# A chunked attention with two MLP layers on one core: the V cast, its write and its gathers stand five to six plan steps further back

## Chip, cores and metric

The kernel runs on one core of a Trainium2 chip. The metric is the device time of one execution in microseconds (us); a time is the median of several runs. Engines are named as in the profile: PE is TensorE (matmuls), PEld its weight loads, DVE VectorE, ACT ScalarE, POOL GpSimd, SP SyncE, whose DMA queue issues the loads, writes and transposes.

## The reference

Three parts follow one another: chunked attention, a leaky MLP, and a sigmoid-gelu MLP. All inputs are float32.

```python
def _attn_ref(q, k, v, mem_k, mem_v):          # 4 batches, 8 heads, 768 rows, 64 wide; 8 memory rows
    ...
    for c in range(nc):                        # chunks of 32 rows
        l_start = max(0, c_start - 16)
        r_end = min(S, c_end + 8)
        k_full = np.concatenate([mem_k, k[:, :, l_start:r_end]], axis=2)
        v_full = np.concatenate([mem_v, v[:, :, l_start:r_end]], axis=2)
        scores = scale * np.matmul(q_c, k_full.transpose(0, 1, 3, 2))
        a = np.exp(scores - np.max(scores, axis=-1, keepdims=True))
        a = a / (np.sum(a, axis=-1, keepdims=True) + 1e-09)
        out[:, :, c_start:c_end] = np.matmul(a, v_full)

def _moe_ref(x, w_in, w_out, alpha):           # 3072 tokens, 512 -> 2048 -> 512
    h = x @ w_in
    return (np.maximum(h, 0.0) + alpha * np.minimum(h, 0.0)) @ w_out

def _moe2_ref(x, w_in, w_out):
    h = x @ w_in
    return (h * (1.0 / (1.0 + np.exp(-1.702 * h)))) @ w_out
```

## The kernel before

**Numbers.** A float32 operand is split into a high and a low half of float16, and a product is made of three float16 products. `cast_hi` (L126) makes the high half on ACT, `sub_lo` (L129) the low half on DVE. The scale of each operand comes from its largest magnitude: `absmax` (L123) on DVE, a pass on ACT that writes to `junk` (L325) for K and Q, and `all_max` (L118 and L119), a small product `mx` on PE and a maximum `ar` on DVE.

**Tiles.** The 3072 tokens are 12 blocks of 256. The first MLP layer runs block by block: a step has a `mlp_g1` (L569: 24 matmuls into `h`), an activation on ACT (L604: `h` to `t`), a DVE part (L607: `t` and `h` to `gf`), the split of `gf` in halves (`g`), and a `mlp_g2` (L649: 24 matmuls into `acc`) for an older `h`. When a block of the MLP is done, `acc` is copied out as `yf` (L685). The weights of both layers are decoded while this runs (`w_load`, L150 and L152; `w_dec`, L191 to L204; `w_sub`, L227; `w_op`, L237 to L239, where `wh` is cast on ACT, combined on POOL and written by SP).

**Attention between the steps.** The attention of a token block stands between the MLP steps of earlier blocks. It loads `kf`, `qf` and `vf` (`att_load`, L300 to L316), finds their maxima, casts K, Q and V, transposes K into `kt` (`att_tk`, L448) and Q (`att_tq`, L434) by DMA, swaps the halves of Q (`att_swap`, L440 and L441), writes V to DRAM as `v_dr` (`att_vw`, L454) and gathers it from there into `vbd` in the form that the product needs, two gathers a head (`att_vr`, L463 and L464). Then come the scores (`att_qk`, L472 and L473), their copy `sc` on ACT (`att_ext`, L487 and L489), the softmax, its transposition to `aT` by DMA (`att_ta`, L525), and two output products `xp` (`att_pv`, L538), whose halves `xt` are the input of the MLP. All of `kf`, `qf`, `vf` and `vbd` are single tiles, used by one block after the other, and so is `kt`. The high and low halves of K and of V are tiles with the same tag, `kv16`, of a pool with one buffer:

```python
        kt = at_p.tile([128, H, 304], F16, tag="kt", name="kt")
        for g, n in ((0, 128), (1, 128), (2, 48)):
            nc.sync.dma_start_transpose(out=kt[:, :, g * 128:g * 128 + n], in_=k16[0:n, g].rearrange("p h t d -> p (h t d)"))
```

A matmul result of `h`, `xp`, `mx` and of `acc` takes one of five PSUM banks.

**What sets the order.** Blocks 0 and 1 have their attention in float32, and that of block 2 is placed by hand (`start`). For blocks 3 to 11 the table `ATT` gives each piece a plan step, relative to the block. Three plan steps belong to one MLP step, and a block has 24. The table writes the program's order only: each engine's own order is then made from it by the scheduler of the framework, so that a piece may end up before or behind work near it. "Block 7" below is the stretch in which K, Q and V of attention block 7 are cast; the two `xp` that stand beside that V cast belong to the block before, and the scores of block 7 follow.

Of the kernel before, what the change touches and what calls it, by code (L numbers as in the profile page):

```python
# [36 lines left out]
def kernel(  # L37
# [15 lines left out]
    B, H, S, D = q.shape  # L53
# [747 lines left out]
    def run_plan(t):  # L801
# [9 lines left out]
        (-7, att_load, 1), (-6, att_load, 0), (-5, att_load, 2),  # L811
        (0, att_max, 1), (1, att_max, 0), (1, att_max, 2), (2, att_all, 0, 3), (4, att_scale, 0, 3),
        (5, att_hi, 1), (6, att_lo, 1), (6, att_hi, 0), (8, att_tk), (7, att_lo, 0), (9, att_tq),
        (9, att_hi, 2), (10, att_lo, 2), (12, att_vw), (13, att_swap),
        *[(15 + h // 2, att_vr, h) for h in range(H)],
        (18, att_qk, 0), (18, att_ext, 0), (20, att_smax, 0), (21, att_qk, 1), (21, att_ext, 1),
        (22, att_exp, 0), (23, att_smax, 1), (24, att_sum, 0), (25, att_exp, 1), (26, att_a16, 0),
        (27, att_sum, 1), (28, att_ta, 0), (29, att_a16, 1), (31, att_ta, 1),
# [222 lines left out]
```

## Time and profile before

| what | value |
| --- | --- |
| median of 3 runs | 1219.28 us (1215.82 to 1219.78) |
| the profiled execution | 1217.3 us, its span 1215.5 us |
| mean granted clock of TensorE, as a share of full speed | 0.946 |
| PE busy | 1086.0 us (89%) |
| DVE busy | 850.9 us (70%) |
| ACT busy | 632.8 us (52%) |
| POOL busy | 632.5 us (52%) |

The page and the trace come from one profiled execution. A span is the time from the first to the last instruction; the execution's own time lies a little above it. Busy shares are averages over stages with different limits, so that the waits of each stage have to be read in its own rows. The attention blocks 3 to 11 lie in the first 680 us. In a row of the timeline, the bracket at the end says how long the engine had been idle before and what it was waiting for; "SPq" is SP issuing a DMA. PEclk of a window is the share of the full clock that TensorE was granted.

### The profile page before, as it was taken

The page shows a single profiled execution, that of the slowest core. Times are in us where ns is not written, and L with a number is a line of the kernel's source. Part 1 is how long each engine was busy: PE and PEld are TensorE (multiplying, and loading weights), DVE is VectorE, ACT ScalarE, POOL GpSimd, SP SyncE. Part 2 cuts the span into 40 slices and gives each one's busy share as a digit, 9 for nine tenths or more (in the row PEclk, how much of TensorE's full clock was granted, in tenths as well). Part 3 has the DMA queues.
Part 4 walks back from the last instruction along what each step waited for, and adds up shares of the span by engine and source line. Part 5 has one row for each costly group of instructions (what it writes and reads, how often), then busy time and mean ns, then how long its engine had stood idle before and what let it go on. Part 6 is the DMA issues. An engine that isn't in the chain of part 4 may idle for free.

```text
span 1215.5 us, 25510 instructions
## 1 busy us (share of the span) xinstructions
PE 1086.0 (89%) x10294; PEld 955.8 (79%) x10294; DVE 850.9 (70%) x1509; ACT 632.8 (52%) x968; POOL 632.5 (52%) x740
## 2 busy tenths in 40 slices
PE   3677879899979898898989999989999898999998
PEld 2665768788869797787979988778788687787887
DVE  6898894687869686776957347767666665766672
ACT  4567546564747556564745344555544544444442
POOL 1244641233607153442607046696876968868763
PEclk8678889999989898998989999999999999999999
DMA  9958238597886969687764515110100100100001
GB/s 204 306 121 187 81 105 159 105 235 162 212 164 194 178 178 219 148 212 168 205 128 126 231 53 233 45 53 10 44 19 19 40 15 18 36 5 15 19 18 36
DMA packets 241318, 142.97 MB, mean 118 GB/s; under 512 B 200176, under 2 KB 220656, under 8 KB 240176
## 3 DMA queue, kind: packets, MB, share of 16 engines
q1 hardware_dynamic: 241200, 141.34, 46.3%
q8 instruction: 81, 1.33, 0.5%
q14 instruction: 37, 0.30, 0.1%
HBM read 86.19 MB, written 33.16 MB: 98 GB/s over the span
## 4 chain that ended last, share of the span: by engine, by line
PE 28%; DVE 24%; POOL 22%; ACT 9%; DMA 7%; issue 6%; SPq 3%; ACTq 0%; POOLq 0%; DVEq 0%
PE h L569 11%; POOL ga L614 10%; PE acc L649 9%; DVE g L129 6%; POOL o L777 4%; PE acc L663 3%; POOL yt L742 3%; ACT g L126 3%; DMA kt<-k 3%; PE x L580 3%; SPq L448 2%; DVE gf L607 2%; DVE wr L204 2%; ACT v L126 2%; DVE wr L198 1%
## 5 line engine op out<-in xcount | busy, mean ns | idle before, releaser
L569 PE MATMUL h<-xt,wbig 128*128 128x256 f16 x2304 | 290.7, 287 | 50.8 <-DVE gf L607 34.0
L569 PEld LDWEIGHTS <-wbig 128*128 128x128 f16 x2304 | 236.1, 103 | 89.8 <-DVE gf L607 34.7
L649 PE MATMUL acc<-g,wbig 128*128 128x256 f16 x2304 | 271.3, 275 | 3.1 <-POOL g L632 1.5
L614 POOL TENSOR_TENSOR ga<-ga 128x128 f32<-128x128 f32 x384 | 212.8, 578 | 114.6 <-DVE ga L612 109.0
L580 PE MATMUL x<-yt,w2i 128*128 128x256 f16 x2016 | 238.1, 275 | 20.2 <-POOL yt L742 12.0
L649 PEld LDWEIGHTS <-wbig 128*128 128x128 f16 x2304 | 226.1, 99 | 31.1 <-issue 3.1
L663 PE MATMUL acc<-w2o,g 128*128 128x256 f16 x2016 | 233.9, 274 | 5.7 <-DVE g L129 2.5
L580 PEld LDWEIGHTS <-w2i 128*128 128x128 f16 x2016 | 198.2, 99 | 50.8 <-issue 20.4
L663 PEld LDWEIGHTS <-g 128*128 128x128 f16 x2016 | 197.5, 98 | 31.7 <-DVE g L129 3.4
L129 DVE SCALAR_TENSOR_TENSOR g<-ga,gk,g 128x896 f16<-128x896 f32 x96 | 122.7, 1289 | 111.3 <-ACT g L126 110.8
L126 ACT ACTIVATE g<-ga,gk 128x896 f16<-128x896 f32 x96 | 98.2, 1036 | 95.1 <-POOL ga L614 95.1
L607 DVE SCALAR_TENSOR_TENSOR gf<-t,oma,h 128x256 f32<-128x256 f32 x192 | 83.1, 473 | 69.5 <-ACT t L604 69.3
L604 ACT ACTIVATE t<-h 128x512 f32<-128x512 f32 x96 | 56.6, 590 | 91.4 <-PE h L569 77.2
L129 DVE SCALAR_TENSOR_TENSOR g<-gf,gk,g 128x512 f16<-128x512 f32 x81 | 82.9, 1024 | 1.8 <-ACT g L126 1.8
L238 POOL TENSOR_TENSOR wh<-wr,wh 128x512 f16<-128x512 f32 x24 | 37.9, 1592 | 79.6 <-ACT wh L237 79.6
L777 POOL TENSOR_TENSOR o<-o 128x256 f32<-128x256 f32 x77 | 74.7, 984 | 6.5 <-ACT o L772 6.0
L227 POOL TENSOR_TENSOR wt<-wr 128x512 f32<-128x512 f32 x16 | 24.2, 1516 | 90.4 <-DVE wr L204 90.2
L611 ACT ACTIVATE ga<-ha,l2t 128x512 f32<-128x512 f32 x48 | 34.4, 717 | 62.6 <-DVE ha L592 62.6
L213 POOL TENSOR_TENSOR wbig<-wr,wbig 128x1024 f16<-128x1024 f32 x16 | 37.1, 2326 | 52.9 <-ACT wbig L208 52.9
L126 ACT ACTIVATE g<-gf,gk 128x512 f16<-128x512 f32 x81 | 57.8, 714 | 0.4 <-DVE gf L607 0.4
L489 ACT COPY sc<-sps 32x504 f32<-32x504 f32 (+2 forms) x112 | 56.2, 502 | 1.0
L612 DVE SCALAR_TENSOR_TENSOR ga<-ga,ha 128x512 f32<-128x512 f32 x48 | 40.1, 834 | 21.9 <-ACT ga L611 21.9
(184 smaller groups left out, 1476.9 us busy)
## 6 DMA issues: line engine op xcount, KB each, us to landing
w<-in_moe_w_in_dram SPq DMA_DIRECT2D x10, 1024.0 KB
w<-in_moe_w_out_dram SPq DMA_DIRECT2D x10, 1024.0 KB
vbd<-v_dr SPq DMA_DIRECT2D x80, 112.0 KB
w2i_dr<-wh SPq DMA_DIRECT2D x28, 256.0 KB
w2o_dr<-wh SPq DMA_DIRECT2D x28, 256.0 KB
w2i<-w2i_dr SPq DMA_DIRECT2D x4, 1792.0 KB
w2o<-w2o_dr SPq DMA_DIRECT2D x4, 1792.0 KB
qf<-in_q_dram SPq DMA_DIRECT2D x24, 256.0 KB
```

What stands on the lines that cost most here:

```text
L126: nc.scalar.activation(out=hi, in_=src, func=ACTF.Copy, scale=s)
L129: nc.vector.scalar_tensor_tensor(out=lo, in0=src, scalar=s, in1=hi, op0=ALU.mult, op1=ALU.subtract)
L489: nc.scalar.copy(d[32 * c:32 * c + 32, ..., 0:WIN], x[32 * c:32 * c + 32, ..., bo + CH * c:bo + CH * c + WIN])
L569: nc.tensor.matmul(out=hp[:, e], lhsT=w[:, wt, o:o + 128], rhs=x[:, xh, kk], start=(n == 0), stop=(n == 3 * KT - 1))
L580: nc.tensor.matmul(out=xs[bank][:, i], lhsT=w[:, o, wt, kk * 256 + c:kk * 256 + c + 128], rhs=yt[sb, yi][:, yh, kk], start=(n == 0), stop= ...
L604: nc.scalar.activation(out=t, in_=hp, func=ACTF.Relu, scale=-1.0)
L607: nc.vector.scalar_tensor_tensor(out=g[:, e], in0=t[:, e], scalar=oma[:, f:f + 1], in1=hp[:, e], op0=ALU.mult, op1=ALU.add)
L612: nc.vector.scalar_tensor_tensor(out=t, in0=t, scalar=1.0, in1=hp, op0=ALU.add, op1=ALU.mult)
L614: nc.gpsimd.tensor_tensor(out=g[:, out_], in0=g[:, x], in1=g[:, y], op=op)
L649: nc.tensor.matmul(out=acc[layer, b][dt // 2][:, dt % 2 * TB:(dt % 2 + 1) * TB], lhsT=w[:, wt, dt * 128:(dt + 1) * 128], rhs=g16[:, gh, e] ...
L663: nc.tensor.matmul(out=acc[layer, b][bank][:, i * 256:(i + 1) * 256], lhsT=g16[:, gh, gs], rhs=w[:, o, wt, p % 2], start=(p == 0 and n == ...
L777: e.tensor_tensor(out=ov[:, out_], in0=ov[:, x], in1=ov[:, y], op=op)
```

## The change

Four entries of the table `ATT` get other plan steps: `att_hi` and `att_lo` of V (9 and 10 become 15 and 16), `att_vw` (12 becomes 18) and the `att_vr` gathers (from 15 becomes from 20). `att_swap` stays at 13, and so now comes ahead of the write of V. Nothing is added or removed, and blocks 0 to 2 are not placed by this table.

```diff
         (5, att_hi, 1), (6, att_lo, 1), (6, att_hi, 0), (8, att_tk), (7, att_lo, 0), (9, att_tq),
-        (9, att_hi, 2), (10, att_lo, 2), (12, att_vw), (13, att_swap),
-        *[(15 + h // 2, att_vr, h) for h in range(H)],
+        (15, att_hi, 2), (16, att_lo, 2), (18, att_vw), (13, att_swap),
+        *[(20 + h // 2, att_vr, h) for h in range(H)],
         (18, att_qk, 0), (18, att_ext, 0), (20, att_smax, 0), (21, att_qk, 1), (21, att_ext, 1),
```

The order that was built from it, engine by engine, is shown at four places. The first pair is ACT in block 7, before, from the cast of Q (`q`) on; `v` is the V cast, `t` and `g` belong to the MLP, and `xt` is the input of a later MLP block.

```order
L126 ACTIVATE q_4826<-qf,blk_143 128x16x64
L604 ACTIVATE t<-h 128x512
L126 ACTIVATE g_4948<-gf,gk_149 128x512
L126 ACTIVATE v_4954<-vf,blk_143 128x1536
L604 ACTIVATE t<-h 128x512
L126 ACTIVATE xt<-xp 128x4x128
L126 ACTIVATE g_5063<-gf,gk_149 128x512
L126 ACTIVATE xt<-xp 128x4x128
L604 ACTIVATE t<-h 128x512
```

The same place of ACT in the change:

```order
L126 ACTIVATE q_4826<-qf,blk_143 128x16x64
L237 CAST wh<-wt 128x512
L604 ACTIVATE t<-h 128x512
L126 ACTIVATE g_4948<-gf,gk_149 128x512
L604 ACTIVATE t<-h 128x512
L126 ACTIVATE v_5131<-vf,blk_143 128x1536
L126 ACTIVATE g_5060<-gf,gk_149 128x512
L126 ACTIVATE xt<-xp 128x4x128 x2
L604 ACTIVATE t<-h 128x512
```

The V cast now stands behind a second `t`; in blocks 9 and 11 it does too. In blocks 4, 6, 8 and 10 it does not. This is ACT in block 8, before:

```order
L126 ACTIVATE q_5607<-qf,blk_144 128x16x64
L604 ACTIVATE t<-h 128x512
L126 ACTIVATE g_5729<-gf,gk_149 128x512
L126 ACTIVATE v_5735<-vf,blk_144 128x1536
L604 ACTIVATE t<-h 128x512
L126 ACTIVATE xt<-xp 128x4x128
```

And ACT in block 8 in the change:

```order
L126 ACTIVATE q_5607<-qf,blk_144 128x16x64
L604 ACTIVATE t<-h 128x512
L126 ACTIVATE g_5729<-gf,gk_149 128x512
L126 ACTIVATE v_5922<-vf,blk_144 128x1536
L604 ACTIVATE t<-h 128x512
L126 ACTIVATE xt<-xp 128x4x128
```

Only the buffer's number differs. The third pair is the DMA queue of SP in block 8, before, from the first swap of Q on: the write of V (`v_dr`), the second swap, the memory rows of `kf` for the next block, `qf`, and the gathers into `vbd`.

```order
L440 DMA q_5886<-q_5733 64x2048
L454 DMA v_dr_101<-v_5735 128x1024 x2
L454 DMA v_dr_101<-v_5735 32x1024
L441 DMA q_5886<-q_5733 64x2048
L313 DMA kf<-in_mem_k_dram 8x8x64
L316 DMA kf<-in_mem_k_dram 8x8x64
L300 DMA qf<-in_q_dram 128x8x64 x2
L464 DMA vbd<-v_dr_101 8x8x128
L463 DMA vbd<-v_dr_101 56x8x128 x2
```

The queue of SP in the change, from the same swap on:

```order
L440 DMA q_5880<-q_5733 64x2048
L441 DMA q_5880<-q_5733 64x2048
L313 DMA kf<-in_mem_k_dram 8x8x64
L316 DMA kf<-in_mem_k_dram 8x8x64
L454 DMA v_dr_101<-v_5922 128x1024 x2
L454 DMA v_dr_101<-v_5922 32x1024
L300 DMA qf<-in_q_dram 128x8x64 x2
L312 DMA vf<-in_v_dram 104x8x64
L312 DMA vf<-in_v_dram 128x8x64
L312 DMA vf<-in_v_dram 32x8x64
L313 DMA vf<-in_mem_v_dram 8x8x64
L463 DMA vbd<-v_dr_101 56x8x128
```

The write stands behind the memory rows of `kf`, and the four loads of `vf` stand ahead of the sixteen gathers; before, they stood behind the last of them. The fourth pair is DVE in block 8's tail, where `vf` of block 9 gets its maximum (`blk_145<-vf`) between the parts of the weight decoding (`wr`) and the MLP (`gf`, `g`). Before:

```order
L198 SCALAR_TENSOR_TENSOR wr<-w_5613,wr 128x1024
L197 TENSOR_SCALAR wr<-wr 128x1024
L607 SCALAR_TENSOR_TENSOR gf<-t,oma,h 128x256 x2
L204 SCALAR_TENSOR_TENSOR wr<-w_5613,wr 128x1024
L129 SCALAR_TENSOR_TENSOR g_6012<-gf,gk_149,g_6012 128x512
L198 SCALAR_TENSOR_TENSOR wr<-w_5642,wr 128x1024
L607 SCALAR_TENSOR_TENSOR gf<-t,oma,h 128x256 x2
L204 SCALAR_TENSOR_TENSOR wr<-w_5642,wr 128x1024
L129 SCALAR_TENSOR_TENSOR g_6107<-gf,gk_149,g_6107 128x512
L123 TENSOR_REDUCE blk_145<-vf 128x1
L499 TENSOR_REDUCE mx<-sc 128x8
```

DVE in the change, from the same first row on:

```order
L198 SCALAR_TENSOR_TENSOR wr<-w_5613,wr 128x1024
L123 TENSOR_REDUCE blk_145<-vf 128x1
L197 TENSOR_SCALAR wr<-wr 128x1024
L607 SCALAR_TENSOR_TENSOR gf<-t,oma,h 128x256 x2
L204 SCALAR_TENSOR_TENSOR wr<-w_5613,wr 128x1024
L129 SCALAR_TENSOR_TENSOR g_5997<-gf,gk_149,g_5997 128x512
```

The maximum over `vf` now comes right behind the first L198, ahead of both pairs of `gf`.

## Rows read from the trace of the kernel before

**Rows 1.** the page, busy time of an engine: us (share of the span) xinstructions

```profile
PE 1086.0 (89%) x10294; PEld 955.8 (79%) x10294; DVE 850.9 (70%) x1509; ACT 632.8 (52%) x968; POOL 632.5 (52%) x740
```

**Rows 2.** the table of waits: engine, line, releaser: us in total, times, longest

```profile
ACT v L126 <- DMA kt<-k: 50.6, 10, 6.9
...
PE h L569 <- DVE gf L607: 34.0, 7, 5.8
```

**Rows 3.** timeline of ACT, block 7: start, us, engine, line, operation, [idle before <-releaser]

```profile
401.48 2.07 ACT L126 ACTIVATE v<-vf,blk 128x1536 f16<-128x1536 f32 x1 [6.63 <-DMA kt<-k]
403.42 0.56 ACT L604 ACTIVATE t<-h 128x512 f32<-128x512 f32 x1
```

**Rows 4.** timeline of DVE, block 7

```profile
405.40 0.86 DVE L607 SCALAR_TENSOR_TENSOR gf<-t,oma,h 128x256 f32<-128x256 f32 x2
```

**Rows 5.** timeline of PE, block 7

```profile
400.61 1.35 PE L538 MATMUL xp<-aT,vbd 128*128 128x32 f16 x48
406.32 4.89 PE L569 MATMUL h<-xt,wbig 128*128 128x256 f16 x24 [4.36 <-DVE gf L607]
```

**Rows 6.** timelines of PE, blocks 9 and 11

```profile
515.21 5.06 PE L569 MATMUL h<-xt,wbig 128*128 128x256 f16 x24 [4.64 <-DVE gf L607]
...
625.16 4.70 PE L569 MATMUL h<-xt,wbig 128*128 128x256 f16 x24 [4.60 <-DVE gf L607]
```

**Rows 7.** the chain that ended last: start, us, what

```profile
468.38 2.62 PE h L569 x24
```

**Rows 8.** windows: us, busy time of each engine, PEclk is the granted clock

```profile
297.00:302.00 5.00, 3.56 (x31) 2.83 (x30) 4.96 (x12) 1.75 (x4) 0.51 (x1) 1.00 0.97 178
407.00:412.00 5.00, 5.00 (x31) 3.80 (x30) 1.20 (x3) 0.70 (x2) 0.00 (x0) 0.64 0.88 231
```

**Rows 9.** timeline of ACT, block 5

```profile
294.07 2.06 ACT L126 ACTIVATE v<-vf,blk 128x1536 f16<-128x1536 f32 x1 [3.93 <-DMA kt<-k]
```

**Rows 10.** timeline of PE, block 5

```profile
291.48 1.35 PE L538 MATMUL xp<-aT,vbd 128*128 128x32 f16 x48
...
295.30 2.78 PE L649 MATMUL acc<-g,wbig 128*128 128x256 f16 x24
...
299.41 0.49 PE L118 MATMUL mx<-eye,wa 128*128 128x128 f32 x2 [1.33 <-DVE xt L129]
...
300.01 2.78 PE L569 MATMUL h<-xt,wbig 128*128 128x256 f16 x24
```

**Rows 11.** timelines of ACT and PE, the tail of block 5

```profile
305.46 1.48 ACT L325 ACTIVATE junk<-kf 128x1536 f16<-128x1536 f32 x1 [6.71 <-DMA kf<-in_mem_k_dram]
...
316.94 0.23 PE L472 MATMUL sps<-kt,q 128*128 128x160 f16 x1 [2.57 <-ACT sc L489]
...
341.56 1.35 PE L538 MATMUL xp<-aT,vbd 128*128 128x32 f16 x48 [0.97 <-DVE ar L119]
```

**Rows 12.** timeline of SP's DMA issues, block 8, and one of block 9

```profile
460.86 2.02 SPq L454 DMA_DIRECT2D v_dr<-v  x3
...
466.34 0.78 SPq L464 DMA_DIRECT2D vbd<-v_dr  x1
...
473.80 2.64 SPq L312 DMA_DIRECT2D vf<-in_v_dram  x3
...
476.49 0.35 SPq L313 DMA_DIRECT2D vf<-in_mem_v_dram  x1
...
500.99 1.54 SPq L525 DMA_TRANSPOSE aT<-a  x1
```

**Rows 13.** timeline of PE, beside the V cast of block 6

```profile
345.37 1.35 PE L538 MATMUL xp<-aT,vbd 128*128 128x32 f16 x48
```

**Rows 14.** timeline of DVE, block 8's tail

```profile
473.00 1.23 DVE L198 SCALAR_TENSOR_TENSOR wr<-w,wr 128x1024 uint32<-128x1024 uint32 x1
```

**Rows 15.** the chain that ended last, two landings

```profile
302.63 2.65 DMA kf<-in_mem_k_dram
...
426.53 7.50 DMA w<-in_moe_w_in_dram
```

## The prediction

> **What bounds the kernel.** I read the page's busy shares first. TensorE (PE) is busy for 1086.0 us, 89% [rows 1], so the time can change only through what PE still waits for, or through the clock at which it runs. I then read the table of waits: the longest wait of PE under one name is `h` (the first product of the MLP, L569) waiting for `gf` on DVE: 34.0 us in seven waits. Its partner is ACT's V cast waiting for the transfer of `kt`, 50.6 us in ten [rows 2]. Third came the timelines, to see that the two are one thing. In block 7 ACT stands idle for 6.63 us until the K transposes have landed, casts V for 2.07 us and only then takes `t` of the next `h` [rows 3]. DVE takes the low half of V, and the `gf` that PE needs follows only at 405.40 [rows 4]. PE has the second output product `xp` of the block before from 400.61 on and starts `h` at 406.32, after 4.36 us of idleness [rows 5]. Blocks 9 and 11 show the same, with 4.64 and 4.60 us [rows 6]. Why V waits for K: both halves' tiles have the tag `kv16` in a pool with one buffer, so the cast may write only when the transposes have read K.
>
> The wait costs more than its idle time. The `h` behind it takes 4.89, 5.06 and 4.70 us for its 24 matmuls [rows 5, 6], where the chain has 2.62 us for the same 24 elsewhere [rows 7]. The granted clock right behind the stall of block 7 is 0.64, that is, TensorE spent much of the stretch at 1.2 GHz [rows 8]. One stall of the three thus costs 4.36 + 2.27, 4.64 + 2.44 and 4.60 + 2.08 us.
>
> **The change, part by part.** The four lines of the table move the V cast and its low half by six plan units, the write by six and the gathers by five. In the order that was built from it:
>
> *Blocks 7, 9 and 11, the V cast.* It now stands behind a second `t` (the first pair of listings, block 7). ACT then waits for `kt` with that `t` already done, and PE has its next `h` and `acc` to run. Removed: idleness 4.36 + 4.64 + 4.60 = 13.60 us and slow clock 2.27 + 2.44 + 2.08 = 6.79 us, together 20.39 us.
>
> *What stands there instead.* The trace has a sample: in block 5 of the kernel before, V already stands behind the second `t` and waits 3.93 us for `kt` [rows 9]. There PE goes on from `xp` to `h` and `acc`, which follow without idleness, and only then waits 1.33 us for `xt` on DVE. The `acc` of 295.30 has issued at 295.30 + 2.62 = 297.92, and the next `h` starts at 300.01 [rows 10]: 2.09 us, in which the small product `mx` also runs. The clock stays at 1.00 over this wait [rows 8]. Three times 2.09 is 6.27 us to take off the gain.
>
> *Given back later.* In block 5 the ACT work behind it is late: the maximum over `kf` waits until 305.46 for the load of the memory rows; later PE waits 2.57 us for the scores' copy on ACT and 0.97 us for a maximum on DVE before the output products [rows 11]. That is 3.54 us which a stalled block does not have. In the changed order part of it has a remedy: on the DMA queue of SP the three writes of V (2.02 us) no longer stand ahead of the memory rows of `kf` [rows 12] (third pair of listings). I take 3.54 − 2.02 = 1.5 us for each of blocks 7 and 9, 3.0 in all. Block 11 prepares no later attention block. Bounds: 0, and 3.54 × 2 = 7.1.
>
> *Block 5 itself* keeps V behind the `t` and gets the same remedy: a gain between 0 and 2.0, since the late tail may be refilled by something else; I take 1.0.
>
> *Blocks 4, 6, 8 and 10, the V cast.* It keeps its place ahead of `t` (second pair of listings), so their stalls stay: 0.
>
> *The write and the gathers.* The sixteen gathers of V into `vbd` run on SP from 466.34 to the first load of `vf` at 473.80 [rows 12]. They now come after the loads of `vf`, so the loads go 7.4 us earlier and the gathers later by the 3.0 us that the four loads issue, and by little else. The output products that read them stand shortly ahead of the `h` of 515.21 [rows 6], over 20 us later: 0. Behind the write on SP stand the loads of `qf` and `vf`. The swaps of `q` and the memory rows go ahead of it, so V's low half has that much more time to be ready, and SP need not stand still for it: 0.
>
> *Transposes.* In block 9 the second transpose of the softmax `aT` (1.54 us of issue for such a one, [rows 12]) now stands between K transposes, and in block 5 too. That delays V, which has cover, and the second output product, which has none: 0 to 1.5 us each. I take 0.5 each, 1.0 in all.
>
> Sum: −20.39 + 6.27 + 3.0 − 1.0 + 1.0 = −11.1 us. From the profiled execution of 1217.3 us (its span is 1215.5) that is 1206.2; the median of the runs, 1219.28, is 2.0 above the profiled one, so the forecast is 1208. After the attention blocks PE runs without such waits, so everything behind shifts together.
>
> With the bounds: the largest gain is −20.39 + 6.27 − 2.0 = −16.1; the smallest, with all of the tail given back and `aT` late twice, is −20.39 + 6.27 + 7.1 + 3.0 = −4.0. Hence 1203 to 1215 for this case, on the median's scale.
>
> **Rivals.**
>
> *The gain is given back (0.22).* The hard evidence against my sum is the period of block 5. From the second `xp` beside its V, at 291.48, to that beside the next block's V, at 345.37 [rows 10, 13] are 53.89 us, and from there to 400.61 [rows 5] 55.24 us with a stall. The block without the stall is only 1.35 us shorter, where a stall of 7 less 2.09 would make it 5. If blocks 7 and 9 behave so, they bring 1.35 each, and block 11, which has no such tail, 4.60 + 2.08 − 2.09 = 4.6: together −7.3, with 1.0 either way for the rest: 1211 to 1213. Against it: the first of block 5's late waits goes back to the load of the memory rows, which the change moves.
>
> *The slower clock stays (0.06).* If the 1.33 us of idleness is enough for the clock to fall each time, 6.8 us of the gain stay away: 1215. Block 5 speaks against it, at 1.00 in the stretch of the wait [rows 8]. The Trainium skill (page "TensorE: Matmul & The Clock Gate", section "A second HAM failure mode: psum-queue depth-cycling") says that short idles between groups of matmuls, as PSUM banks are cycled, can be enough to make the clock go back and forth. Block 5's row does not bear it out here: its short idle left the clock up.
>
> *Slower (0.12): DVE is held by the loads of V.* The maximum over `vf` now stands directly behind the first L198 of the weight decoding and ahead of `gf` (fourth pair of listings); before, it stood behind two pairs of `gf`. By block 8's rows DVE comes to it at 473.00 + 1.23 = 474.2 [rows 14]. The loads of `vf` now start at 466.34 and their four issues take 3.0 us [rows 12], to 469.3. With a landing like the 2.65 us of the memory rows of `kf` they are there at 472.0 and nothing waits; with one like the 7.50 us of a weight load they come at 476.8 [rows 15], and DVE, with `gf` behind, stands 2.6 us. In seven blocks that is 18.2 us, and the sum becomes +7.1: 1226. It decides at 11.1 / 7 = 1.6 us of PE wait per block. For it: the DMA engines' share is high, 0.97 and 0.88, in the two windows that I read beside such stretches [rows 8]. Against it: it takes a landing at the far end, and in block 5 ACT waited 6.71 us for a load [rows 11] without PE standing still at once.
>
> *More is gained (0.08).* If an earlier tail also shortens the even blocks' stalls, say by 2 us of the four, 8 us more: 1200.
>
> *No effect (0.10).* The built order moves the cast in only three of the blocks; if ACT is held there by something that I do not see, the stall moves one `h` further and keeps its price: 1217 to 1221.
>
> **How the numbers follow.** My case has 0.42, and 1208 with a range of its own of 1203 to 1215. The range reaches up over the given-back case and most of no effect, to 1219, and down to 1199, which takes in the larger gain: outside are the slower case and about half of no effect. About 0.3% (3.7 us) is what a measurement can tell from no change here: faster means below 1215.6. My case 0.40, given back 0.20, the larger gain 0.08 and the clock 0.03 make faster 0.71. Same is 0.09 of no effect and what of the others lies near the old time, 0.16. Slower is 0.13.
>
> **What would show it.** Right: in the profile after, PE's wait for `gf` on DVE falls from seven times to four and from 34.0 to about 20.4 us; ACT's row of V in blocks 7, 9 and 11 stands behind two `t` and still waits for `kt`; the `h` after the second `xp` starts at once and takes 2.62 us; the granted clock there is 1.00; some 1.3 us of waiting for `xt` stand one `acc` later. The load of the memory rows of `kf` is issued about 2 us sooner after the K transposes. Wrong: new waits of PE for `sc` or `ar` of 3 to 4 us in the tails of blocks 7 and 9 (given back); DVE's maximum over `vf` waiting for its load with `gf` behind it (slower); an `h` of 4 to 5 us behind a short wait (the clock). The prediction breaks most easily at the tail, for which I have one block as a sample.

## The result and the profile after

The changed kernel takes 1230.08 us (median of 4 runs, 1228.91 to 1231.3), the kernel before, measured beside it, 1219.53 us (4 runs, 1215.82 to 1220.68). The ratio over all executions is 1.0092, with a 95% interval of 1.0068 to 1.0116; the medians are 10.6 us apart. The change makes the kernel slower. The forecast was 1208, with a range up to 1219. The profiled execution took 1229.92 us, its span 1228.1 us, at a mean granted clock of 0.947 (0.946 before).

The page's busy line, as in [rows 1]:

```profile
PE 1093.2 (89%) x10294; PEld 960.4 (78%) x10294; DVE 855.5 (70%) x1509; ACT 633.0 (52%) x968; POOL 635.6 (52%) x740
```

Every engine runs the same number of instructions. PE is busy 7.2 us longer, so some of its matmuls took longer, and idle for the other 5.4 us of the 12.6 between the two profiled executions. The table of waits of the changed kernel, to be held against [rows 2]:

```profile
ACT junk L325 <- DMA v_dr<-v: 42.4, 8, 7.0
ACT v L126 <- DMA kt<-k: 41.3, 10, 6.9
```

The wait of the V cast for `kt` has become shorter (50.6 before). The first line is new: ACT's pass over `kf` waits 42.4 us for a transfer. Before, the longest wait of these passes was 10.9 us in six, for the memory rows of `kf`. The row names the write of V, but the pass reads `kf` alone, and the write is issued directly behind the memory rows. By the semaphores in the trace these rows land 0.1 to 0.3 us ahead of the pass in each of blocks 4 to 10, so the pass waits for them. PE's waits, from the same table cut to PE:

```profile
PE h L569 <- DVE gf L607: 20.7, 4, 6.2
...
PE xp L538 <- DVE ar L119: 7.6, 5, 2.7
PE sps L472 <- ACT sc L489: 7.5, 4, 3.5
PE acc L649 <- DVE gf L607: 6.2, 2, 4.8
...
PE mx L118 <- DVE xt L129: 3.4, 2, 1.7
```

The stall at the V cast went from seven times and 34.0 us to four and 20.7, as forecast. Of the other four, `xp` behind `ar` and `sps` behind `sc` had 1.0 us once and 2.6 us once before. What left as one kind of wait has come back as several.

**Block 7, where the stall was to go.** The timeline of ACT, to be held against [rows 3]:

```profile
408.95 2.08 ACT L126 ACTIVATE v<-vf,blk 128x1536 f16<-128x1536 f32 x1 [2.62 <-DMA kt<-k]
...
412.57 0.60 ACT L604 ACTIVATE t<-h 128x512 f32<-128x512 f32 x1
418.75 1.49 ACT L325 ACTIVATE junk<-kf 128x1536 f16<-128x1536 f32 x1 [5.58 <-DMA v_dr<-v]
...
423.34 1.06 ACT L325 ACTIVATE junk<-qf 128x1024 f16<-128x1024 f32 x1 [2.40 <-DMA qf<-in_q_dram]
...
424.39 2.35 ACT L191 ACTIVATE wr<-w,wcs 128x1024 f32<-128x1024 f32 x2
```

And that of PE, to be held against [rows 5]:

```profile
402.99 1.38 PE L538 MATMUL xp<-aT,vbd 128*128 128x32 f16 x48 [1.64 <-DVE ar L119]
404.21 4.45 PE L649 MATMUL acc<-g,wbig 128*128 128x256 f16 x24
408.50 1.35 PE L538 MATMUL xp<-aT,vbd 128*128 128x32 f16 x48
409.70 2.78 PE L569 MATMUL h<-xt,wbig 128*128 128x256 f16 x24
```

Behind the second `xp`, at 408.50, PE goes straight on, at full speed: `h` takes 2.78 us where it took 4.89. But ahead of the first `xp` it has waited 1.64 us, and the `acc` behind that wait took 4.45 us. And ACT, once V is cast, waits 5.58 and then 2.40 us for loads before it comes to the first pass of the weight decoding (`wr`). Further on in the same block PE stands still once more, for a `gf` whose `t` stands on ACT behind a cast that waits for a DMA. ACT first, then PE:

```profile
444.69 1.14 ACT L237 CAST wh<-wt 128x512 f16<-128x512 f32 x2 [2.10 <-DMA w2o_dr<-wh]
445.86 0.60 ACT L604 ACTIVATE t<-h 128x512 f32<-128x512 f32 x1
```

```profile
447.41 2.95 PE L649 MATMUL acc<-g,wbig 128*128 128x256 f16 x13 [4.79 <-DVE gf L607]
...
452.39 2.78 PE L569 MATMUL h<-xt,wbig 128*128 128x256 f16 x24
```

The `acc` that begins at 447.41 takes until 452.39, 4.98 us, where 24 matmuls take 2.62 us in [rows 7]. The stall with its slow restart is back, 38 us further on.

**Block 8, where the stall was to stay.** It has stayed: `h` starts at 470.33 after 4.67 us of waiting for `gf` and takes 5.30 us. Here ACT and SP show what the moved write does. First ACT in the changed kernel:

```profile
465.51 2.05 ACT L126 ACTIVATE v<-vf,blk 128x1536 f16<-128x1536 f32 x1 [5.34 <-DMA kt<-k]
...
476.55 1.49 ACT L325 ACTIVATE junk<-kf 128x1536 f16<-128x1536 f32 x1 [7.00 <-DMA v_dr<-v]
...
478.04 0.58 ACT L604 ACTIVATE t<-h 128x512 f32<-128x512 f32 x1
```

Then the DMA queue of SP there, to be held against [rows 12]:

```profile
469.38 0.49 SPq L440 DMA_DIRECT2D q<-q  x1
...
470.55 0.66 SPq L313 DMA_DIRECT2D kf<-in_mem_k_dram  x1
471.25 0.97 SPq L316 DMA_DIRECT2D kf<-in_mem_k_dram  x1
472.26 1.54 SPq L454 DMA_DIRECT2D v_dr<-v  x3
```

The same stretch of SP in the kernel before, where the write stands between the swaps:

```profile
460.28 0.49 SPq L440 DMA_DIRECT2D q<-q  x1
...
463.63 0.49 SPq L313 DMA_DIRECT2D kf<-in_mem_k_dram  x1
464.17 1.01 SPq L316 DMA_DIRECT2D kf<-in_mem_k_dram  x1
```

And of ACT in the kernel before:

```profile
465.63 0.60 ACT L604 ACTIVATE t<-h 128x512 f32<-128x512 f32 x1 [6.02 <-PE h L569]
...
466.96 1.49 ACT L325 ACTIVATE junk<-kf 128x1536 f16<-128x1536 f32 x1
```

The memory rows are issued 1.2 us after the first swap instead of 3.4, as forecast. The pass over `kf` starts 7.2 us after that swap, where it was 6.7 us before: in this block nothing has landed sooner. It is the only one of the seven. From the start of the first swap (L440) to that of the pass over `kf`, in us, worked out from the timelines of SP and ACT:

```
block     4     5     6     7     8     9     10
before   8.25  6.76  8.14  6.72  6.68  7.98  7.93
after    6.68  5.99  6.18  4.89  7.17  6.61  6.30
```

The rows for block 7, before and then after; the pass after is shown above, at 418.75:

```profile
406.05 0.47 SPq L440 DMA_DIRECT2D q<-q  x1
412.77 1.48 ACT L325 ACTIVATE junk<-kf 128x1536 f16<-128x1536 f32 x1 [0.27 <-DMA kf<-in_mem_k_dram]
```

```profile
413.86 0.47 SPq L440 DMA_DIRECT2D q<-q  x1
```

The order on ACT has changed as well. In block 8, where before ACT took `t` first and then the pass without a wait, it now stands 7.00 us in front of the pass, with `t` behind it.

**The period.** From the second `xp` beside one V cast to that beside the next, in us, for blocks 4 to 11, worked out from the starts in the timelines of PE (block 11 has no V cast after it; its period ends with the last second `xp`):

```
block     4      5      6      7      8      9      10     11     sum
before  54.72  53.89  55.24  54.27  54.33  54.72  55.28  53.65  436.10
after   58.91  52.92  58.48  55.80  58.16  54.63  56.46  50.89  446.25
        +4.2   -1.0   +3.2   +1.5   +3.8   -0.1   +1.2   -2.8   +10.15
```

The loss is in blocks 4, 6, 8 and 10, which kept their stall: 12.4 us. Blocks 7 and 9 lost the stall and are no shorter. A difference of 1 or 2 us in a single block should not be read closely: two of the experiments below are in effect the same two orders executed once more, and there block 5 takes 55.95 us (cast_only, the order of before) and 51.70 (write_gathers, the order of the change). Their sums, 438.57 and 447.62, and the 11.6 us between them in blocks 4, 6, 8 and 10 repeat the picture. Of the 12.6 us between the profiled executions, 10.15 lie in these eight periods.

### The profile page after: what moved, and what is told of

The parts are those of the page before. It is cut to its first block, busy times and chain, and to the rows that moved or that the text cites. A ratio compares the mean times of both kernels' runs of the same rounds, so it can differ in the third digit from the quotient of the medians.

```text
span 1228.1 us, 25516 instructions
## 1 busy us (share of the span) xinstructions
PE 1093.2 (89%) x10294; PEld 960.4 (78%) x10294; DVE 855.5 (70%) x1509; ACT 633.0 (52%) x968; POOL 635.6 (52%) x740
## 4 chain that ended last, share of the span: by engine, by line
DVE 24%; PE 23%; POOL 22%; DMA 10%; ACT 8%; issue 7%; SPq 4%; ACTq 0%; POOLq 0%; DVEq 0%
POOL ga L614 10%; PE h L569 9%; PE acc L649 8%; DVE g L129 6%; POOL o L777 5%; POOL yt L742 3%; ACT g L126 3%; DMA q<-q 2%; PE acc L663 2%; DVE gf L607 2%; PE x L580 2%; SPq L448 2%; DMA kt<-k 2%; DVE hb L592 1%; DVE ga L612 1%
## 5 line engine op out<-in xcount | busy, mean ns | idle before, releaser
L569 PE MATMUL h<-xt,wbig 128*128 128x256 f16 x2304 | 285.2, 283 | 38.0 <-DVE gf L607 20.7
L649 PE MATMUL acc<-g,wbig 128*128 128x256 f16 x2304 | 277.9, 279 | 9.5 <-DVE gf L607 6.2
L580 PE MATMUL x<-yt,w2i 128*128 128x256 f16 x2016 | 237.8, 275 | 20.7 <-POOL yt L742 13.0
L238 POOL TENSOR_TENSOR wh<-wr,wh 128x512 f16<-128x512 f32 x24 | 34.3, 1439 | 66.7 <-ACT wh L237 66.7
L227 POOL TENSOR_TENSOR wt<-wr 128x512 f32<-128x512 f32 x16 | 27.6, 1723 | 75.4 <-DVE wr L204 39.1
```

The source lines that it names most:

```text
L569: nc.tensor.matmul(out=hp[:, e], lhsT=w[:, wt, o:o + 128], rhs=x[:, xh, kk], start=(n == 0), stop=(n == 3 * KT - 1))
L580: nc.tensor.matmul(out=xs[bank][:, i], lhsT=w[:, o, wt, kk * 256 + c:kk * 256 + c + 128], rhs=yt[sb, yi][:, yh, kk], start=(n == 0), stop= ...
L649: nc.tensor.matmul(out=acc[layer, b][dt // 2][:, dt % 2 * TB:(dt % 2 + 1) * TB], lhsT=w[:, wt, dt * 128:(dt + 1) * 128], rhs=g16[:, gh, e] ...
```

## The experiments

Eighteen kernels were run, in five groups, each group beside the kernel before (medians of 1217.54, 1219.59, 1219.86, 1218.13 and 1218.22 us). Behind each median stands its ratio to the kernel before, with the 95% interval; the ratio is taken over all executions, so that it can lie up to 0.2% from that of the medians. The diffs show the lines that decide, not every line.

### Which part of the change costs the time

**cast_only** moves the V cast as the change does and puts everything behind it so that the write and the gathers keep their places:

```diff
-        (9, att_hi, 2), (10, att_lo, 2), (12, att_vw), (13, att_swap),
-        *[(15 + h // 2, att_vr, h) for h in range(H)],
+        (15, att_hi, 2), (16, att_lo, 2), (16.2, att_vw), (16.4, att_swap),
+        *[(16.5 + 0.3 * h, att_vr, h) for h in range(H)],
```

> Only the V cast and its low half get the change's plan steps (15, 16); the write, the swap and the gathers follow within one step, ahead of the loads of vf, so that their order stays the old one. Theory A (the gathers and the loads of vf decide): the built order is that of before, 1219, within 3. Theory B (the write behind the memory rows decides): the same, 1219. Rival (a V cast placed later costs or gains by itself): 1208 to 1214 if the removed stalls pay, 1224 or more if it costs.

**write_gathers** leaves the cast where it was and moves the rest:

```diff
+        (9, att_hi, 2), (10, att_lo, 2), (18, att_vw), (13, att_swap),
+        *[(20 + h // 2, att_vr, h) for h in range(H)],
```

> Only the write (18) and the gathers (from 20) are moved; the V cast keeps its old plan steps 9 and 10. Theories A and B: 1230, within 3, since the built order is that of the whole change, the V cast's new place in blocks 7, 9 and 11 with it. Rival (the cast's own step does it): 1219.

**write_late** is the change with the gathers directly behind the write (`18.1 + 0.1 * h`); the built order then has V where the kernel before has it, with the stalls of blocks 4 and 6 to 11.

> The whole change, but the gathers follow the write within a step, ahead of most loads of vf. The V cast then stays ahead of t in every block, so all seven stalls stay; the write still stands behind the memory rows of kf, and ACT's maximum over kf ahead of a t. Theory A: 1219, within 4. Theory B: 1228 or more.

**gathers_late** moves the gathers alone, to `20 + h // 2`.

> Only the gathers are moved (from 20); the write keeps its place, so SP has the old order up to qf, then the loads of vf ahead of the gathers. DVE's maximum over vf comes early, as in the change; the V cast stands behind t in block 9 only, beside block 5. Theory A (vf early and the weight load behind the gathers hold DVE in the tails): 1226 to 1234. Theory B: 1217 to 1221.

Measured: cast_only 1218.61, ratio 1.0001 (0.9983 to 1.0019). write_gathers 1229.52, 1.0086 (1.0063 to 1.0109). write_late 1229.12, 1.0082 (1.0053 to 1.0110). gathers_late 1233.69, 1.0115 (1.0091 to 1.0138). The order built for cast_only is that of the kernel before, but for one DMA issue of SP, and that for write_gathers is that of the change: the cast stands where it stands whatever its own plan step, which fits a scheduler that places a piece when its operands are there. So the change is the move of the write and the gathers, and V's new place behind `t` in blocks 7, 9 and 11 comes out of that as well. write_late, which takes the gathers along with the write, and gathers_late each cost as much as the whole, so the two do not add up. The waits of write_late:

```profile
PE h L569 <- DVE gf L607: 37.1, 7, 6.8
...
ACT junk L325 <- DMA v_dr<-v: 35.6, 7, 6.7
```

And those of gathers_late:

```profile
PE h L569 <- DVE gf L607: 30.8, 6, 6.1
...
ACT junk L325 <- DMA kf<-in_mem_k_dram: 22.5, 7, 7.4
```

In write_late all seven stalls are there, and the time is that of the change: whether three stalls go or none makes no difference that the intervals show. In gathers_late, where the write stands ahead of the memory rows, ACT's wait has their name; it is a wait for loads in either kernel.

**even_blocks** gives blocks 3, 4, 5, 6, 8 and 10 the changed steps and leaves 7, 9 and 11 at the old ones.

```diff
+        for u in ATT((15, 16, 18, 20) if nb not in (7, 9, 11) else (9, 10, 12, 15)):
```

> The change in blocks 3, 4, 5, 6, 8 and 10 alone; 7, 9 and 11 have the old plan steps, and in the built order V yet stands behind t there. Theory (each tail pays for the moved write and gathers beside it, the removed stall pays back): tails of 4, 6 and 8 lose as in the change, those of 7 and 9 less: 1219 to 1227. Rival (the loss comes from the odd blocks, where V stands behind t): 1210 to 1216 here.

Measured: 1225.94, 1.0066 (1.0042 to 1.0089). V stands behind `t` in blocks 7, 9 and 11 here too, although their steps are the old ones: its place depends on what the blocks ahead of it do. Most of the loss comes without a moved step in these three blocks.

### Is it the maximum over vf

With the loads of `vf` ahead of the gathers, DVE takes the maximum over `vf` (1.75 us) in the middle of the weight decoding. **vmax_act_before** and **vmax_act_change** give it to ACT, on the kernel before and on the change:

```diff
-VACT = ()
+VACT = tuple(range(3, 12))
```

> The kernel before, with the maximum over vf of blocks 3 to 11 taken on ACT (a pass like those for K and Q) and not on DVE. Theory (DVE's queue is the tail's chain, and in before it ends just in time): the stalls stay, 1214 to 1220. Rival (DVE does not matter in the tails): 1219, within 2, or slower by ACT's 1.5 us a block.

> The change, with the maximum over vf of blocks 3 to 11 on ACT. In its built order V stands ahead of t again in all blocks but none, so the seven stalls are there as in before. If the early maximum over vf on DVE is what costs: 1217 to 1222. If the write behind the memory rows and the weight loads behind the gathers cost: 1227 or more, as in write_late.

**gathers_late_vmax_held** and **change_vmax_held** hold it behind the decoding instead, by a small DVE operation that reads `wr` and writes to where the maximum goes:

```diff
+            if nb > 4:
+                nc.vector.tensor_scalar(out=bs(nb, 2), in0=lazy["wr"][:, 0:1], scalar1=0.0, scalar2=None, op0=ALU.mult)
```

> As gathers_late (only the gathers from step 20), with the maximum over vf of blocks 5 to 11 held on DVE behind the weight decoding's second L204 by a small operation that reads its result; the DMA queue's order stays that of gathers_late, vf and the weight loads' place with it. If the early maximum over vf, ahead of the decoding that feeds POOL, makes the 14 us of gathers_late: 1217 to 1224. If the weight loads behind the gathers, or the loads of vf ahead of them, make it: 1229 or more.

> The change, with the maximum over vf of blocks 5 to 11 held on DVE behind the second L204 of the weight decoding; V stands ahead of t in the built order of blocks 4 and 6 to 11, so seven stalls are there, and ACT's maximum over kf stands ahead of a t. If the early maximum over vf makes the loss of the change: 1217 to 1222. If it makes a part, as in gathers_late: 1223 to 1227. If the loads' landing and the maximum over kf make it: 1228 or more.

Measured: vmax_act_before 1226.35, 1.0051 (1.0035 to 1.0067). vmax_act_change 1228.04, 1.0083 (1.0054 to 1.0112). gathers_late_vmax_held 1225.55, 1.0058 (1.0039 to 1.0077), against 1.0115 without the hold. change_vmax_held 1229.59, 1.0085 (1.0058 to 1.0111). The early maximum is about half of what the gathers alone cost; gathers_late_vmax_held thus lies between the two ranges that were written down. On the change, holding it back brings nothing that can be measured. But there, and in vmax_act_change, the built order has V ahead of `t` in blocks 7, 9 and 11 again, and PE waits for `gf` seven times (37.7 and 37.2 us), so that neither is the change with this one thing undone. vmax_act_before is slower than the theory had it (1214 to 1220); its rival had named the 1.5 us that the pass costs on ACT.

### Is the stall worth anything by itself

**v_behind_t** is the kernel before with V forced behind `t` in blocks 3 to 11: a small DVE operation reads `t` and makes the scale that the V cast uses, with the write and the gathers at their old steps.

```diff
+        if i == 2 and nb > 2:
+            nc.vector.scalar_tensor_tensor(out=bs(nb, 15), in0=lazy["t"][:, 0, 0:1], scalar=0.0, in1=bs(nb, 5), op0=ALU.mult, op1=ALU.add)
+            cast_hi(hi, vf, bs(nb, 15))
+            return
-        (9, att_hi, 2), (10, att_lo, 2), (12, att_vw), (13, att_swap),
+        (11, att_hi, 2), (11.2, att_lo, 2), (12, att_vw), (13, att_swap),
```

> The kernel before, with one thing forced: the V cast of blocks 3 to 11 takes its scale through a small DVE operation that reads the t before it, so V stands behind that t in every block; plan steps 11, 11.2 for the cast and its low half, the write and the gathers as before. If the terms of the prediction hold, seven stalls go (34.0 us idle, 14.0 of slow clock), 7 x 2.09 come for them and 6 x 1.5 in the tails: 1219 - 24 = 1195. Theory (the work from the maxima to the casts is a chain without slack, which ends at the output products, so what is won at V is lost there): 1212 to 1222, with new waits of xp for ar and of the scores for sc.

Measured: 1229.39, 1.0092 (1.0059 to 1.0124). PE's waits:

```profile
PE sps L476 <- ACT sc L493: 16.4, 5, 4.3
...
PE xp L542 <- DVE ar L119: 9.4, 6, 2.7
...
PE h L573 <- DVE gf L612: 6.3, 3, 2.9
```

The stall has gone almost everywhere (6.3 us of 34.0 left), and the kernel is as slow as the change, slower than either number written down for it. Its mean granted clock, 0.954, lies among those of the kernel before (0.940 to 0.958 over its executions). The sum of the eight periods is 447.05. This falls on the price that the prediction put on a stall: it is real at its place, and taking it away does not shorten the blocks that have a tail. Block 11, which prepares no later attention block, does get shorter, 48.25 us against 53.65.

### What sets the length of a block

**less_pe** takes PE work away: the third of the three partial products of `h` is left out, 8 of 24 matmuls (7.0 us a block by [rows 7]).

```diff
+    TWO = ((0, 0), (0, 1))
-            for (wt, xh) in TRI:
+            for (wt, xh) in TWO:
```

> The kernel before, with the third of the three half products left out of the first product of layer 1 (16 in place of 24 matmuls in each h; 7 us of PE a block). Theory (the loop sets a block's time): the 436 us from the second output product of block 3 to that of block 11 shrink by under 15, and the end by what lies outside of them, some 15 to 20: 1185 to 1205. Rival (PE sets it): by 56 there and 1150 or less in all.

**no_row_max** takes work from the others: in blocks 3 to 11 the softmax goes without the row maximum (two of 0.68 us a block on DVE) and its subtraction (two of 1.0 to 1.5 us on POOL).

```diff
+        if nb not in F32B and nb > 2:
+            return
```

> The kernel before, without the subtraction of the row maximum in the softmax of blocks 3 to 11 (two maxima on DVE and two subtractions on POOL left out a block, some 1.4 and 4 us of work). V stays ahead of t and the seven stalls stay. Theory (a loop from the K transposes over the loads, the maxima, the decoding on DVE, POOL's run and the scales back to the K cast sets a block's time, and PE has slack in it): 2 to 5 us a block, 1185 to 1206. Rival (PE with its stalls sets it): 1216 to 1220.

Measured: less_pe 1161.41, 0.9527 (0.9506 to 0.9547); its second `xp` go from 335.8 to 585.1 in five periods, 49.9 us each, where the same five took 54.8 before, from 345.37 [rows 13] to 619.21 (−4.9 of 7.0). no_row_max 1209.91, 0.9930 (0.9908 to 0.9952), with the stalls kept (29.6 us in eight); its eight periods sum to 428.76 (−0.9 a block). The waits of PE in less_pe:

```profile
PE acc L650 <- DVE g L129: 20.8, 7, 4.0
PE acc L650 <- ACT g L126: 12.9, 9, 3.5
```

Both kernels missed both of the numbers that were written down for them. In less_pe the built order differs too, with no `t` between the casts of Q and V in blocks 5 to 11. Taking work from either side shortens the block, and neither gives all of it as time: with less PE work PE waits for the halves `g` instead. This fits a block that is a loop through PE and the others, and not the sum of PE's work and its stalls.

### The order on ACT behind V

Behind V, the kernel before has two `t` ahead of the pass over `kf` in most blocks; v_behind_t has none in blocks 4, 6, 8 and 10. **write_late_kmax_late** and **change_t_first** put the pass over `kf` behind a `t`; the first by a small DVE operation on `t`, the second by letting one `t` of a block accumulate into the place where the maximum goes:

```diff
-            nc.scalar.activation(out=t, in_=hp, func=ACTF.Relu, scale=-1.0)
+            cnt = lazy["n"] = lazy.get("n", 0) + 1
+            nb, r = divmod(cnt - -16, 8)
+            acc = {"accum_out": bs(nb, 1)} if r == 0 and 3 < nb < NB else {}
+            nc.scalar.activation(out=t, in_=hp, func=ACTF.Relu, scale=-1.0, **acc)
```

> As write_late, with ACT's maximum over kf of blocks 4 to 11 made to come behind a t (a small DVE operation on its result column reads t). In the built order both maxima, of kf and of qf, then stand behind the two decoding passes (L191), so that the decoding no longer waits for the memory rows of kf. Theory (the first L204 of the decoding sets when the K cast comes): the 11 us of write_late go, 1208 to 1221. Rival (the write's place in the DMA queue costs by itself): 1227 or more.

> The change, with ACT's maximum over kf of blocks 4 to 11 made to follow the second t behind V (the t writes the result column first); V stays behind t in blocks 7, 9 and 11, the maximum over vf stays early. If a t that stands behind the wait for the loads is what costs: 1217 to 1224. If it is not: 1228 or more.

**change_both** and **v_behind_t_both** have the same and the held maximum over `vf` besides, on the change and on v_behind_t.

> The change with both: the maximum over vf held behind the decoding, the t ahead of the maximum over kf. What is left of the change is the DMA queue's order (write behind the memory rows, gathers behind the loads of vf). If the two orders on DVE and ACT make the loss: 1217 to 1222. If the DMA queue's order makes it by later landings: 1227 or more.

> v_behind_t with both orders restored (the maximum over vf behind the decoding, a t ahead of the maximum over kf), so that no stall at V is left and the tail stands nearly as in before. If the tails' order was what ate the gain of v_behind_t: 1195 to 1212. If the work from V to the next K cast has no slack whatever its order: 1217 or more, with PE waiting for sc and ar.

Measured: write_late_kmax_late 1230.20, 1.0092 (1.0068 to 1.0116). change_t_first 1233.52, 1.0113 (1.0079 to 1.0147). change_both 1233.44, 1.0113 (1.0082 to 1.0144). v_behind_t_both 1226.40, 1.0070 (1.0043 to 1.0097). On the change this order gains nothing; 1.0113 lies above the change's 1.0092, with intervals that overlap. In change_both the pass over `qf` still stands ahead of the decoding and V ahead of `t` in blocks 7, 9 and 11, so it is neither the whole order of before nor the change without its stalls. In v_behind_t_both the waits are:

```profile
ACT junk L328 <- DMA qf<-in_q_dram: 47.0, 11, 8.3
...
PE sps L479 <- ACT sc L496: 34.7, 7, 7.3
```

PE's 34.0 us of waiting for `gf` have become 34.7 us of waiting for the scores' copy on ACT, which stands behind a pass that waits for `qf`. So the last two kernels put the decoding (L191) ahead of both passes (`- -15` in the lines above): **decode_first** on the kernel before, **decode_first_v_behind_t** on v_behind_t with the held maximum.

> The kernel before, with ACT's maxima over kf and qf of blocks 4 to 11 made to come behind the two decoding passes (L191); the DMA queue's order and the V cast's place are those of before, with all seven stalls. If the wait for the loads ahead of the decoding holds up the way from V to the next K cast: 1205 to 1214. If the late maxima, which the K cast needs too, hold it up as much: 1216 to 1226.

> v_behind_t_both, with the decoding passes ahead of both maxima on ACT, so that ACT need not wait for the load of qf before them. No stall at V is left. If v_behind_t_both lost its gain only since ACT waits for qf ahead of the decoding and the scores' copies: 1195 to 1214, the wait of PE for sc (34.7 us there) under 15. If the gain has no way out whatever the order on ACT: 1218 or more.

Measured: decode_first 1221.46, 1.0027 (1.0015 to 1.0040). decode_first_v_behind_t 1219.16, 1.0012 (0.9993 to 1.0031). In the second, PE's waits are headed by this:

```profile
PE acc L660 <- DVE gf L618: 24.0, 6, 5.9
```

And ACT behind V shows the order, in block 8:

```profile
461.26 2.09 ACT L126 ACTIVATE v<-vf,blk 128x1536 f16<-128x1536 f32 x1 [1.61 <-DMA kt<-k]
...
469.14 2.37 ACT L191 ACTIVATE wr<-w,wcs 128x1024 f32<-128x1024 f32 x2 [2.85 <-DVE wcs L184]
...
472.17 1.48 ACT L328 ACTIVATE junk<-kf 128x1536 f16<-128x1536 f32 x1
```

With the decoding ahead of the loads that ACT would wait for, V behind `t` costs nothing any more: 1.0070 has become 1.0012, some 7 us, with intervals that do not touch. It also gains nothing over the kernel before. With no stall at V in any block, PE waits 24.0 us somewhere else, for `gf` ahead of `acc`. In the kernel before, the same order of ACT made it slower, not faster. Block 11 alone keeps its gain, with 46.98 us. Of the kernels that leave no work out, none was faster than the one before.

## Why the prediction was wrong

**The stalls of blocks 7, 9 and 11: right at their place.** The wait for `gf` fell from seven times to four and by 13.3 us (13.6 forecast), V stands behind two `t`, and `h` runs at 2.78 us in block 7. Forecast net of the short waits were 4.5, 5.0 and 4.6 us for the three; the periods gave −1.5 (longer), 0.1 and 2.8. Of the 21.3 us between the forecast and the measured sum of the periods, 12.4 lie in the even blocks, 8.0 in blocks 7 and 9 and 1.8 in block 11, less the 1.0 that the transposes had been given as a term of their own.

**"Given back later", 1.5 each for blocks 7 and 9: the first step that failed.** Everything was given back, 6.1 and 4.9 us. This is the first rival, and its evidence, the period of block 5, was the better witness than the sum over block 5's rows, though one period is a thin one (55.95 in cast_only, no shorter than block 6). The waits named for it, `xp` for `ar` and `sps` for `sc`, came, but in these two blocks they are the smaller part. In block 7 PE waits 0.67 us for `sc`, none for `ar`, and 4.79 us for `gf` ahead of the `acc` at 447.41, with a slow restart; in block 9 it waits 1.71 us for `xt`, 1.66 for `sc`, 1.45 for `gf` and 1.14 for `ar`. Most of the 7.6 us of `xp` behind `ar` lies at the end of blocks 4, 6 and 8 (2.71, 1.64 and 1.88 us). v_behind_t gives the stalls' gain back without the moved write, so a cast behind `t`, with the order that is built around it, is enough for that.

**"Blocks 4, 6, 8 and 10: 0": the step that decided.** They cost 12.4 us. The argument was that the cast keeps its place, so nothing changes there. But three other things of the same tail moved, and write_late, which has a stall in all seven blocks, pays the whole price without any gain. The distance from a V cast to the next K cast shows it, in us, for blocks 4 to 10, worked out from the starts of the two casts on ACT:

```
block     4     5     6     7     8     9     10
before   45.0  43.8  43.5  45.0  45.9  45.3  43.4
after    49.2  43.4  47.0  47.5  48.6  43.5  46.2
```

From the K cast to the next V are 9 to 12 us in either kernel. So the loss sits between V and the next K. The end of the weight decoding on DVE parts this distance once more. From the start of the V cast to that of the decoding's last part, the second L204, in us, worked out from the timelines of ACT and DVE:

```
block     4     5     6     7     8     9     10
before   23.7  21.8  21.9  22.8  23.7  22.9  21.8
after    28.0  21.8  26.0  26.0  26.4  20.4  24.5
```

The rows for block 7, before and then after (V at 401.48 and 408.95):

```profile
424.33 2.17 DVE L204 SCALAR_TENSOR_TENSOR wr<-w,wr 128x1024 uint32<-128x1024 uint32 x1
```

```profile
434.93 2.04 DVE L204 SCALAR_TENSOR_TENSOR wr<-w,wr 128x1024 uint32<-128x1024 uint32 x1
```

From there to the next K cast are 21 to 23 us in either kernel. So the blocks lost their time ahead of this point: in blocks 4, 6, 7, 8 and 10 ACT comes to the first L191 0.4 to 3.8 us later behind V, and in blocks 5 to 10 the maximum over `vf` stands among the parts of the decoding. This is read from the rows, not shown by an experiment. It does not work the other way: in decode_first_v_behind_t the last L204 of these blocks starts 15 to 17 us behind V, and the next K still comes 44 to 47 us behind V.

**"The write and the gathers: 0", and the 2.0 us of remedy: failed.** The remedy came for the most part: behind the swap the pass over `kf` starts 0.8 to 2.0 us sooner in six of the seven blocks. It was worth nothing: the decoding behind the pass came not sooner but, in five of the seven, later behind V. In block 8 the rows themselves came no sooner: SP has issued them at 472.22, and ACT's pass starts 4.3 us later; before it started 1.8 us after they were issued, and without a wait. The Trainium skill (page "DMA: Bandwidth & Descriptors", section "Latency and other measured facts") says that an access to HBM takes longer under high load, 0.2 us on average and 2 us then. The windows of block 8 agree in direction, with a DMA share, as the profile counts it, of 1.27 and 1.11 in the two windows from 466 to 476, and 0.88 and 1.08 before, from 461 to 471. No run here parts such an access from the waiting behind other transfers. The order of the gathers is not free either: gathers_late alone costs 1.0115, half of it through the place of the maximum over `vf`.

**Block 5, −1.0: right in sign** (−1.0 measured; with the repeats, between −1.0 and −4.3). That the number itself came out is luck, given this spread. **Transposes, 1.0:** PE waits 0.64 us for an `aT` in block 9 and 0.21 in block 5; right in size.

**The slower rival** had the sign and nearly the size (1226 against 1230), but not by its mechanism: in block 8 DVE takes the maximum over `vf` at 484.57 without a wait for its load, and the table of waits lists no more than 1.0 us, once, for a maximum of this kind behind a transfer. Its bound, the order of DVE, mattered otherwise, as a piece of 1.75 us ahead of `gf`.

**The slower clock: the prediction weighed it too lightly.** It said that block 5's row did not bear out what the Trainium skill says there (page "TensorE: Matmul & The Clock Gate", section "A second HAM failure mode: psum-queue depth-cycling"). The changed kernel has rows of both kinds. PE in blocks 9 and 11:

```profile
530.77 0.49 PE L118 MATMUL mx<-eye,wa 128*128 128x128 f32 x2 [1.71 <-DVE xt L129]
531.36 2.78 PE L569 MATMUL h<-xt,wbig 128*128 128x256 f16 x24
...
641.87 0.49 PE L118 MATMUL mx<-eye,wa 128*128 128x128 f32 x2 [1.71 <-DVE xt L129]
642.46 4.41 PE L569 MATMUL h<-xt,wbig 128*128 128x256 f16 x24
```

And the windows of the two, with the granted clock behind the busy times:

```profile
530.00:535.00 5.00, 4.12 (x36) 3.58 (x37) 3.93 (x18) 0.37 (x2) 0.00 (x0) 1.00 1.05 254
...
641.00:646.00 5.00, 4.03 (x23) 3.00 (x24) 4.90 (x26) 1.16 (x2) 0.00 (x0) 0.74 0.72 204
```

The same wait of 1.71 us left the clock at 1.00 once and was followed by 0.74 the other time; there `h` takes 1.6 us longer than in block 9. In block 11, which missed its forecast by 1.8 us, that is nearly all of it. Over the whole kernel `h` takes 5.5 us less than before (285.2 against 290.7) and `acc` 6.6 us more (277.9 against 271.3), by the pages: the slow groups went from `h` to `acc`.

**What stays open.** Which single link sets the time from V to the next K was not settled: holding one maximum, moving the passes behind `t` and moving the decoding each gave a part on one kernel and nothing or a loss on another, and most of these edits moved other pieces of the built order too. In block 8 a maximum over a weight load waits 2.85 us on DVE where it waited 0.20, and the load is issued 29.2 us behind the V cast where it was 26.6; this was seen and not tested. Work for PE to fill the stall, and tiles of their own for the halves of K and V, were not tried.

## What to carry to other kernels

A stall that recurs once in a loop is worth what the loop's period loses without it, and a block that already lacks the stall can show this: compare periods, over more than one execution, before adding up idle times. Where a scheduler places work by readiness, read from the built order what has really moved, and give every piece that has moved a price, also in the blocks in which the argued piece stayed. Work that is ready can go ahead of a piece that waits for a load on the same engine, but only a run tells what it is worth: putting the decoding ahead of the passes gave 7 us on one kernel here and cost 3 us on another.

## What was not expected of the hardware

The memory rows of `kf` were issued about 2 us earlier against their swap. The pass that needs them began 0.8 to 2.0 us sooner after the swap in six blocks and 0.5 us later in block 8, in a stretch with a DMA share of 1.1 to 1.3. An idle time of 1.6 to 1.9 us of PE was followed by groups of 4.4 us for 24 matmuls twice (`acc` at 404.21, `h` at 642.46) and by groups at full speed, 2.78 us, twice (`h` at 531.36, `acc` at 519.03).
